# Modulation gates taken as columns through DRAM, six score sets, and Q/K weights loaded in column parts

## The chip, the cores and the metric

One Trainium2 chip, one core of it. The metric is the device time of one execution in microseconds (us). The executions of a kernel are compared with executions of the kernel before on the same chip in the same rounds.

The engines: TensorE (PE, with its weight loads PEld), VectorE (DVE), ScalarE (ACT), GpSimd (POOL), and SyncE (SP), which here issues all transfers (DMA) in one queue, in order (q1 on the pages: 50946 of the 50990 packets of the kernel before).

## The reference, cut to what matters

Shapes: `x` is 1 x 2048 x 640, 32 heads of 20, a causal window of 256, feed-forward width 1536, all bf16.

```python
mod = (silu(c) @ w_mod).reshape(1, 6, 1, 640)
sa, ca, ga, sb, cb, gb = (mod[:, i] for i in range(6))
h = layernorm(x) * (1 + ca) + sa
x = x + ga * attention(h, wqkv, wo)          # ga: the first gate
h = layernorm(x) * (1 + cb) + sb
x = x + gb * ((sigmoid(h @ w_gate) * (h @ w_up)) @ w_down)   # gb: the second gate
```

Two of the six modulation vectors are gates. The kernel multiplies them into the weights `wo` and `w_down`. For that each gate must stand as one row of 640, repeated on all 128 partitions (`gbc`).

Of the kernel before, what the change touches and what calls it, by code (L numbers as in the profile page):

```python
# [13 lines left out]
D = 640  # L14
H = 32
DH = 20
# [10 lines left out]
ENGS = ("pe", "act", "dve", "pool", "sp")  # L27

# [21 lines left out]
class Tile:  # L50
# [18 lines left out]
    @property  # L69
    def ap(self):  # L70
        return self.pool.aps[self.slot]

# [6 lines left out]
class Prog:  # L79
# [69 lines left out]
    def schedule(self):  # L149
# [35 lines left out]
        while placed < n:  # L185
# [62 lines left out]
            if o.isdma:  # L248
# [8 lines left out]
                hbm = max(acc + 0.8, hbm) + o.nbytes / 300e3  # L257
# [36 lines left out]
    def emit(self):  # L294
# [72 lines left out]
    "": "290 430 340 608 722 1953 1410 1740 303 468 448 570 1053 1093 711 721 823 490 280 320 510 -476 -138 -724 "  # L367
        "-544 -539 -489 -71 134 716 878 906 1114 630",
    "dma": "192",
    "x0": "-493",  # L370
    "x1": "122",
    "wm0": "289 373 247 331 163",
    "wqk": "593 396 748 863",
    "x2": "458",
    "x3": "571",
    "wv": "655",
    "warm": "1688 1731 1808 1817 1860 1903 608 651 694 2096 2118 1733 1755 1777 2206 2358 2303 2246 2268 2290",
    "c": "495",
    "modc": "715 854 921 802 892 636 867 881 894 907",
    "pad": "3909 5019",  # L380
    "stats@l0": "513 601 1331 1473",
    "aggr@l0": "2080 2100 2841 2972",
    "eps@l0": "570 1327",
    "pow@l0": "-460 1299",
    "xh@l0": "581 712 1726 1402",
    "ptr@l0": "645 747 685 403 767 1330 1387 1279 1412 1259",
    "hT0@l0": "-1511 -1721 -2114 -2170 -1702 -1156 -1042 -850 -674 -894",
    "projd@q0": "1459 1470 1482 1494 1506 1237 1305 1415 1444 1491 1823 1518 1340 1435 1447 1293 1341 1352 1352 "
        "1399 1518 1589 1601 1590 1625 2666 2618 2630 2642 2571 1951 1963 1974 1986 1998 2426 2437 2429 2441 2550 "
        "2526 2511 2535 2355 2665 3078 3090 3336 3113 3125 3206 3336 3348 3359 3371 3451 3494 3553 3581 3577 3218 "  # L390
        "3230 3241 3253 3265 3483 3589 3193 3632 3644 3420 3506 3518 3530 3542 3277 3289 3300 3312 3324",
    "evd@q0": "2246 1511 2380 1296 2117 3495 4441 3413 3670 3148 3408 4055 3755 4850 3604 3508",
    "projv0@q0": "2260 2288 1873 1900 1213 1644 2741 2766 3764 3791 3668 3856 4701 4729 4525 4553",
    "evv@q0": "2354 2393 1710 2835 1322 1753 3711 4640",
    "projq0@q0": "2687 2709 2129 2151 2074 2096 2238 2329 2019 2041",
    "evqk@q0": "990 1105 925 1294 996 1338 1786 1967 1544 1160",
    "qkw@q0": "3031 2588 2554 2692 2363 2752 3157 3354 2856 2528",
    "qkr@q0": "3818 3083 3041 3524 3860 3571 3609 3693 3567 3399 3545 3686 3902 3944 3776 4139",
    "projk0@q0": "2361 421 2810 2832 2990 3012 2482 2258 2184 2206",
    "wo@w": "5221 1685 2696 2459",  # L400
    "x4@l1": "1684",
    "x5@l1": "-3",
    "x6@l1": "1246",
    "x7@l1": "3007",
    "stats@l1": "2240 2112 1966 2328",
    "aggr@l1": "423 516 255 -869",
    "eps@l1": "2142",
    "pow@l1": "3115",
    "xh@l1": "4779 4659 4831 2815",
    "ptr@l1": "3146 3045 2947 2887 2864",  # L410
    "hTe@l1": "2501 1738 2392 2111 4012",
    "wm1@w": "2662 1477 2296 3998 3038",
    "modb@w": "5742 5769 6219 6194 9058 9085 9030 9126",
    "@w": "4934 5232 6126 8243 8298 8559",
    "modc@w": "6315 6328 6302 6457 6368 9167 9189 9422 9478 9491",
    "wos@w": "6411 6577 6699 6833 6728",
    "wm2@w": "7685 7139 7415 7878 6150",
    "wg@w": "9448 4001 8420 3092 5176 9902 4628 9836 9534 8922",
    "projq1@q1": "3934 4020 3977 4085 5851 5936 4888 4838 6069 6112",
    "evqk@q1": "3777 4175 6139 4611 5808 4684 4738 5207 5034 5620",  # L420
    "qkw@q1": "4228 4290 6482 4014 6064 4471 4208 5263 5164 5741",
    "qkr@q1": "6890 7188 6349 6092",
    "projk1@q1": "4327 4477 4243 4286 5074 5117 4769 4944 5455 5521",
    "projv1@q1": "5714 5810 3720 3747 4231 4452 5402 5429 6892 7082 6288 6578 6001 6416 5182 5209",
    "evv@q1": "4642 3829 4662 5328 7148 6250 6241 7971",
    "x8@l2": "3314",
    "x9@l2": "3422",
    "x10@l2": "3048",
    "x11@l2": "3443",
    "stats@l2": "3891 4057 3646 3734",  # L430
    "aggr@l2": "4037 4165 3871 4145",
    "eps@l2": "4247",
    "pow@l2": "4171",
    "xh@l2": "4506 4626 4486 4217",
    "ptr@l2": "5227 5028 4898 5341 5475",
    "hTe@l2": "1073 908 666 1262 1783",
    "score0@a0": "1587 1795 2920 3179 3392 3665 3841 3869",
    "exp0@a0": "1694 1895 3065 3145 3184 3341 3892 4158",
    "mask0@a0": "4936 3068 3790 3335 4505 4438 4716 4628 3044 2925 3411 2747 3019 3203 5634 5399",
    "pv0@a0": "3432 3463 3601 4187 4620 4640 5283 5302",  # L440
    "tr1@a0": "5924 6672 7198 7764",
    "recip@a0": "3621 4407 5110 4826",
    "divide@a0": "3979 4364 4932 5660",
    "tr2@a0": "4185 4710 4919 6259",
    "n_ow@a0": "5213 6164",
    "oT@a0": "6082 6356 6361 6345",
    "score1@a1": "4404 4669 5018 5331 5596 5245 5528 5800 6736 7022 7312 7614",
    "exp1@a1": "4449 4393 5090 5124 5510 6070 6380 6445 6882 7427 7533 7834",
    "mask1@a1": "4743 5195 5262 5195 5418 5835 4866 5475 5761 5641 6444 6173 6522 6399 6332 6367 6748 6682 6939 "
        "7006 7526 7100 7288 7192 7551 7460 7507 7740 8042 7976 8109 7387",  # L450
    "pv1@a1": "5628 5530 5556 6368 6412 6438 7546 7553 7579 7807 7833 8171",
    "tr1@a1": "5386 5962 7203 7796",
    "recip@a1": "4011 4674 6196 6643",
    "divide@a1": "5752 6555 7709 8385",
    "tr2@a1": "5958 6916 7740 8448",
    "n_ow@a1": "7195 8682",
    "oT@a1": "9194 9236 10033 9163",
    "wd@w": "12285 10761 11898 11749 12135 10910",
    "wds@w": "12996 12902 10989 10990 12482 12308 12113 11826 12880 13137 11378 11361",
    "x0@o0": "5965",  # L460
    "x1@o0": "6847",
    "wo0@o0": "7054 7191 7344 7029 7123 7150 7900 7927",
    "res1@o0": "7130 7632 7232 7943",
    "stats@o0": "7846 8181",
    "aggr@o0": "7925 8208",
    "eps@o0": "8321",
    "pow@o0": "9688",
    "xh@o0": "8529 8729",
    "transp@o0": "8417 8754",
    "modu@o0": "8694 9092 9256 8648 8699",  # L470
    "mlpg0@m0": "10485 10507 10678 10700 10865 10914 11728 11141 11403 11425 11513 11535 11665 11895 12392 12676 "
        "12168 12452 12206 12562 12586 12749 12836 12962",
    "mlpu0@m0": "10616 10638 10726 10748 10942 10962 11167 11189 11451 11483 11603 11625 11971 11993 12291 12382 "
        "12478 12575 12665 12687 12631 12653 12899 12921",
    "tanh@m0": "7042 7268 7797 11349 10492 11023 11809 11844 12141 12143 11761 12611",
    "glu@m0": "10926 10599 8433 11355 11611 11767 12164 12064 10375 10683 10350 10944",
    "down0@m0": "13436 13545 13678 13732 13787 14083 12989 13141 13490 13195 11887 11941",
    "res2@m0": "13250 13519 13183 13201",
    "out@m0": "13049 12362",
    "x2@o1": "4105",  # L480
    "x3@o1": "9866",
    "wo1@o1": "9957 9984 10240 10575 10880 11094 9482 11171",
    "res1@o1": "8885 9322 9602 9782",
    "stats@o1": "8874 9750",
    "aggr@o1": "11300 11788",
    "eps@o1": "12157",
    "pow@o1": "11951",
    "xh@o1": "12415 12471",
    "transp@o1": "13000 12774",
    "modu@o1": "12818 13129 13489 13438 13432",  # L490
    "mlpg1@m1": "13962 14048 14595 14617 15103 15125 15587 15609 16496 16230 16359 16381 16476 14690 14820 16667 "
        "16739 16761 16977 16989 17128 17150 17219 17293",
    "mlpu1@m1": "14481 14596 15097 15066 15154 15176 16214 16297 16314 16336 16544 16566 16634 16656 16744 16766 "
        "16983 17005 17092 17156 17244 16315 16453 15824",
    "tanh@m1": "13668 14197 14019 15261 15826 16069 16094 16320 16359 16578 16821 16672",
    "glu@m1": "14177 14047 14044 15218 15965 16207 16804 16480 16687 16752 16927 16694",
    "down1@m1": "16373 17507 17895 17950 18004 18210 17389 17689 17744 17798 18059 18113",
# [194 lines left out]
def build(nc, A_x, A_wqkv, A_wo, B_x, B_w_gate, B_w_up, B_w_down, c, w_mod, out, S=2048):  # L692
# [55 lines left out]
    def R(name):  # L748
        return Res(name)
# [69 lines left out]
    for b in range(2, 4):  # L819
        x0[b] = load_x(p_x0, b, 0.31 + 0.001 * b)  # L820
# [618 lines left out]
```

## The kernel before: the parts that the change touches

The kernel is a list of operations with read and write sets. A small list scheduler in the kernel file, with a cost model and a table of priorities, places them on the five engines when the kernel is built; the order on each engine is then fixed. A gate is made by multiplying `silu(c)`, repeated over 128 columns (`silubc`), with the columns of `w_mod`: every partition gets the same row, so nothing has to be broadcast afterwards.

```python
def mod_bc(wm, c0, factor, prio):
    for half in range(2):
        ps = Tile(p_M, "modb")
        pairs = [(ps[:, 0:320], silubc[:, kt, :], wm[:, kt, c0 + half*320 : +320]) for kt in range(5)]
        pe_chain(ps, 320, pairs, ...)                       # 5 matmuls of 320 columns
        gbc[:, half*320 : +320] = ps * factor               # VectorE
# ... shifts and scales are made as columns, [128, 5]:
def mod_cols(wm, c0, ps, prio):                             # w_mod is the stationary side
    for kt in range(5):
        for cg in range(5):
            mm(ps[:, cg*64 : +64], wm[:, kt, c0 + cg*128 : +128], silubc[:, kt, 0:64])
# ... the first Q/K weights come in two halves of 320 columns:
def load_wqk(half):
    for w in (wq, wk): dma(w[:, :, half*320 : +320], wqkv_src[...])
# ... [cut]: the scores of the first chunk go through exp in eight sets of 384 columns
```

(The code is abridged: index arithmetic and arguments are cut.)

The softmax here doesn't subtract the row's maximum and nothing guards it: scores larger than these inputs give would overflow.

## Time and profile before

| kernel before | |
|---|---|
| median of 6 runs, lowest and highest | 343.79 us, 342.9 to 345.37 |
| span of the profiled execution | 339.9 us |
| TensorE busy | 97% |
| TensorE's share of the chain that ended last | 92% |
| transfers under 512 bytes | 16513 of 50990 packets |

How to read it: the span is cut into 40 equal slices; a digit is the busy share of a slice in tenths (9 is 90% or more), and for PEclk the clock granted to TensorE in tenths of full speed. In the views, L864 is a line of kernel.py, often that of a helper. `x` are input blocks, `hT` and `h2T` the normalised inputs transposed (attention, feed-forward), `stg` results on their way out, `dq`, `dk` and `doc` the copies of Q, K and the attention output in DRAM, `QT`, `KT` and `oT` what is read back of them, `big` w_mod and later the products of the feed-forward, `wgu` w_gate and w_up, `wd` w_down.

```profile
PE   7799989999999999998999999999999999999996
...
PEclk9999999999999999999999999999999999999999
```

TensorE is full from end to end (97% busy) and its clock does not drop (1.00 granted up to the last matmul).

### The profile page before, as it was taken

The page shows a single profiled execution, that of the slowest core. Times are in us where ns is not written, and L with a number is a line of the kernel's source. Part 1 is how long each engine was busy: PE and PEld are TensorE (multiplying, and loading weights), DVE is VectorE, ACT ScalarE, POOL GpSimd, SP SyncE. Part 2 cuts the span into 40 slices and gives each one's busy share as a digit, 9 for nine tenths or more (in the row PEclk, how much of TensorE's full clock was granted, in tenths as well). Part 3 has the DMA queues.
Part 4 walks back from the last instruction along what each step waited for, and adds up shares of the span by engine and source line. Part 5 has one row for each costly group of instructions (what it writes and reads, how often), then busy time and mean ns, then how long its engine had stood idle before and what let it go on. Part 6 is the DMA issues. An engine that isn't in the chain of part 4 may idle for free.

```text
span 339.9 us, 9584 instructions
## 1 busy us (share of the span) xinstructions
PE 330.0 (97%) x3813; PEld 201.2 (59%) x3813; DVE 227.6 (67%) x493; ACT 226.9 (67%) x229; POOL 178.4 (52%) x301
## 2 busy tenths in 40 slices
PE   7799989999999999998999999999999999999996
PEld 2577646655555656564765433466545446788884
DVE  4576599999776889646977446398746874554432
ACT  1377878888888888896887798956678851022230
POOL 5132564797666999555675566656656850010000
PEclk9999999999999999999999999999999999999999
DMA  6966689889987752472064101302740122112101
GB/s 211 353 202 181 191 235 257 288 270 209 231 282 253 224 194 41 151 226 60 2 180 115 48 31 65 111 3 40 162 123 12 49 22 72 44 35 41 39 3 39
DMA packets 50990, 44.99 MB, mean 132 GB/s; under 512 B 16513, under 2 KB 46850, under 8 KB 50946
## 3 DMA queue, kind: packets, MB, share of 16 engines
q1 hardware_dynamic: 50946, 44.38, 45.4%
q8 instruction: 30, 0.49, 0.6%
q14 instruction: 14, 0.11, 0.1%
HBM read 28.90 MB, written 12.19 MB: 121 GB/s over the span
## 4 chain that ended last, share of the span: by engine, by line
PE 92%; DMA 4%; SPq 1%; DVE 1%; ACT 1%; issue 0%; ACTq 0%; DVEq 0%
PE M L842 74%; PE S L843 8%; PE O L843 7%; PE M L843 3%; DMA big<-in_w_mod_dram 2%; DMA oT<-doc 1%; SPq L764 1%; DMA doc<-On 1%; ACT hT L984 0%; DVE x L937 0%; DVE V L1020 0%; DVE hT L1005 0%; ACT stg L1019 0%; DVE x L1316 0%; DVE big L1306 0%
## 5 line engine op out<-in xcount | busy, mean ns | idle before, releaser
L1188 ACT ACTIVATE E<-S 128x2048 bf16<-128x2048 f32 (+1 forms) x64 | 118.0, 1844 | 20.9 <-PE S L843 19.6
L842 PE MATMUL M<-h2T,wgu 128*128 128x256 bf16 (+1 forms) x720 | 114.6, 309 | 0.0
L842 PEld LDWEIGHTS M<-h2T,wgu 128*128 128x128 bf16 x720 | 67.2, 98 | 36.6 <-issue 5.5
L1199 POOL TENSOR_SCALAR_AFFINE_SELECT E<-E 128x512 bf16<-128x512 bf16 x89 | 59.9, 683 | 23.3 <-ACT E L1188 21.6
L1201 POOL TENSOR_SCALAR_AFFINE_SELECT E<-E 128x512 bf16<-128x512 bf16 x78 | 50.4, 655 | 31.8 <-ACT E L1188 27.5
L1306 DVE SCALAR_TENSOR_TENSOR big<-sig,M 128x256 bf16<-128x256 f32 (+1 forms) x72 | 36.4, 506 | 41.7 <-PE M L842 20.2
L1304 ACT ACTIVATE sig<-M 128x256 f32<-128x256 f32 (+1 forms) x72 | 32.4, 452 | 44.1 <-PE M L842 43.5
L842 PE MATMUL M<-wd,big 128*128 128x320 bf16 x384 | 56.5, 299 | 0.0
L842 PEld LDWEIGHTS M<-wd,big 128*128 128x128 bf16 x384 | 36.5, 98 | 16.0 <-issue 1.7
L843 PE MATMUL S<-QT,KT 20*128 20x256 bf16 (+2 forms) x832 | 36.2, 258 | 0.0
L926 DVE BATCH_NORM_STATS2 st<-x 128x6 f32<-128x320 bf16 x64 | 27.3, 477 | 7.2 <-DMA x<-in_A_x_dram 7.1
L1249 DVE STREAM_TRANSPOSE T<-O 128x512 f32<-128x512 f32 x32 | 22.6, 708 | 12.6 <-PE O L843 12.5
L843 PEld LDWEIGHTS S<-QT,KT 20*128 20x128 bf16 x832 | 12.3, 92 | 26.5 <-ACT E L1188 9.4
L1316 DVE TENSOR_TENSOR x<-M,x 128x320 bf16<-128x320 f32 x32 | 15.5, 484 | 18.3 <-PE M L842 17.8
L842 PE MATMUL M<-wv,hT 128*128 128x320 bf16 x160 | 27.4, 300 | 0.0
L842 PE MATMUL M<-wo,oT 128*128 128x320 bf16 x160 | 25.8, 300 | 1.5 <-DMA oT<-doc 1.4
L932 POOL TENSOR_SCALAR st<-st 128x2 f32<-128x2 f32 (+1 forms) x11 | 3.0, 274 | 40.4 <-DVE st L929 40.4
L842 PE MATMUL M<-hT,wk 128*128 128x512 bf16 (+1 forms) x100 | 23.1, 354 | 1.1 <-DVE V L1020 1.0
L1258 DVE STREAM_TRANSPOSE On<-Tn 128x512 bf16<-128x512 bf16 x32 | 22.5, 704 | 0.5
L842 PE MATMUL M<-hT,wq 128*128 128x512 bf16 (+1 forms) x100 | 22.7, 356 | 0.0
L843 PE MATMUL O<-E,V 128*32 128x256 bf16 (+2 forms) x568 | 21.1, 262 | 0.0
L1019 ACT ACTIVATE stg<-M 128x512 bf16<-128x512 f32 (+1 forms) x31 | 16.5, 534 | 6.6 <-PE M L842 6.2
(85 smaller groups left out, 386.3 us busy)
## 6 DMA issues: line engine op xcount, KB each, us to landing
x<-in_A_x_dram SPq DMA_DIRECT2D x32, 160.0 KB, 4.1
big<-in_w_mod_dram SPq DMA_DIRECT2D x15, 320.0 KB, 5.5
doc<-On SPq DMA_DIRECT2D x16, 256.0 KB, 2.2
KT<-dk SPq DMA_DIRECT2D x6, 512.0 KB, 5.1
QT<-dq SPq DMA_DIRECT2D x6, 512.0 KB, 4.7
out_dram<-x SPq DMA_DIRECT2D x16, 160.0 KB, 1.8
wgu<-in_B_w_gate_dram SPq DMA_DIRECT2D x5, 384.0 KB, 4.1
dq<-stg SPq DMA_DIRECT2D x15, 128.0 KB, 3.2
```

The source lines that it names most:

```text
L842: return e.matmul(o, l, r, start=st, stop=sp, skip_group_check=True)
L843: return e.matmul(o, l, r, start=st, stop=sp, tile_position=tp, skip_group_check=True)
L926: ins = e.bn_stats(v(bi * 12 + j * 6, 6), src[bi].ap[:, j * 320:(j + 1) * 320])
L1019: return e.activation(dst(), src(), ACT.Copy)
L1188: A("act", lambda e, eng, E=E, Sp=Sp, ncol=ncol: e.activation(E.ap[:, :, 0:ncol], Sp.ap[:, :, 0:ncol], ACT.Exp, scale=SM_SCALE), c_act(4 * ...
L1199: return e.affine_select(ap, ap, pattern=[[0, 4], [1, 128]], compare_op=ALU.is_ge, fill=0.0, base=0, channel_multiplier=-1)
L1201: return e.affine_select(ap, ap, pattern=[[0, 4], [-1, 128]], compare_op=ALU.is_ge, fill=0.0, base=-1, channel_multiplier=1)
L1249: A("dve", lambda e, g: e.transpose(T1.ap[:], O.ap[:]), 0.71, reads=[O.r()], writes=[T1.r()], prio=4, tag="tr1")
L1258: A("dve", lambda e, g: e.transpose(On.ap[:, half * 512:half * 512 + 512], Tn.ap[:]), 0.71, reads=[Tn.r()], writes=[On.r(half)], prio=7, t ...
L1304: A("act", lambda e, g, pg=pg, sg=sg: e.activation(sg.ap[:, 0:W], pg.ap[:, 0:W], ACT.Tanh, scale=0.5), c_act(W), reads=[pg.r()], writes=[s ...
L1306: A("dve", lambda e, g, pu=pu, sg=sg, ft=ft: e.scalar_tensor_tensor(out=hv(ft), in0=sg.ap[:, 0:W], scalar=1.0, in1=pu.ap[:, 0:W], op0=ALU. ...
L1316: A("dve", lambda e, g, ps=ps, bi=bi, half=half: e.tensor_tensor(x1[bi].ap[:, half * 320:half * 320 + 320], ps.ap[:, 0:320], x1[bi].ap[:, ...
```

## The change

Its intent: take work from TensorE and from the head of the kernel. (1) Both gates are made as columns like the shifts and scales (25 matmuls of 64 columns in place of 10 of 320), and a transfer to DRAM and back turns the column into a broadcast row. (2) The scores of the first chunk go through exp in six sets of 512 columns in place of eight of 384. (3) The first Q/K weights come in three column parts. (4) The modulation columns use PSUM banks that belong to the scores and are free at that time. (5) The priorities were searched anew, with a cost model that got a DRAM bandwidth for each kind of transfer.

```diff
+    CUTS = [0, 172, 332, D]
+    def load_wqk(part):
+        c0, c1 = CUTS[part], CUTS[part + 1]          # ... one wq and one wk transfer for each part
...
     def mod_bc(wm, c0, factor, prio):
-        for half in range(2):
-            ... five matmuls of 320 columns, then gbc[:, half] = ps * factor on VectorE
+        gd = dram(f"gate{c0}", [D])
+        col = mod_cols(wm, c0, ps, prio)
+        A("dve", ... tensor_scalar(gcol[:], col(), factor, None, op0=ALU.mult) ...)
+        dma(gd.rearrange("(t p) -> p t", p=128), gcol[:], 1280, ..., nd=640, tag="gw")
+        dma(gbc[:], bass.AP(gd.tensor, gd.offset, [[0, 128], [1, D]]), 163840, ..., tag="gr")
...
-    psA, psA2 = Tile(p_M, "modA"), Tile(p_M, "modA2")
+    psA, psA2 = Fixed(p_S.aps[0][:, 1, :], "psA"), Fixed(p_S.aps[0][:, 2, :], "psA2")
...
+        if a == 0:    # six score sets, three for each four groups of heads
...
 TIMES = { ... all priorities replaced ... }
```

`gcol` is [128 partitions, 5], and element (p, t) goes to place 128 t + p of one run of 1280 bytes: 640 single elements of 2 bytes.

## The prediction

> **What bounds the kernel now.** I read the page first: busy time by engine, then the chain that ended last.
>
> ```profile
> span 339.9 us, 9584 instructions
> PE 330.0 (97%) x3813; PEld 201.2 (59%) x3813; DVE 227.6 (67%) x493; ACT 226.9 (67%) x229; POOL 178.4 (52%) x301
> ...
> PE 92%; DMA 4%; SPq 1%; DVE 1%; ACT 1%; issue 0%; ACTq 0%; DVEq 0%
> ```
>
> TensorE (PE) is the bound: 97% busy, 92% of the chain, every other engine at two thirds or less. So a part of the change counts only if it alters what PE executes, or how long PE waits. "Busy" says nothing of density, so next I took the timeline of PE in its undisturbed end and divided durations by counts.
>
> ```profile
> 10.40 1.34 PE L842 MATMUL M<-silubc,big 128*128 128x64 bf16 x40 [1.01 <-DMA big<-in_w_mod_dram]
> ...
> 318.06 12.50 PE L842 MATMUL M<-h2T,wgu 128*128 128x256 bf16 x113
> 330.39 6.68 PE L842 MATMUL M<-wd,big 128*128 128x320 bf16 x48
> ```
>
> Start to start (a run's length less the tail of its last matmul) this gives 29 ns for 64 columns, 109 ns for 256, 136 ns for 320, and in other rows 216 ns for 512. The small tiled matmuls (scores, P times V, direct projection) run four at a time, and where PE goes over between full-array, row-tiled and column-tiled work, the start of the next piece comes some 100 ns later than these figures (312 instead of 216 ns after a 512-column matmul). I summed counts by these figures: 294.8 us of work without warm-up, and 237 changes of tiling at 0.1 us = 23.7 us. That is 318 of 340 us. The rest: 13.2 us before the first projection (1.9 us of listed work lies there), 2.8 us after the last matmul, and waits of PE. The waits view of PE names them:
>
> ```profile
> PE M L842 <- DMA big<-in_w_mod_dram: 2.0, 2, 1.0
> PE M L842 <- DMA oT<-doc: 1.4, 1, 1.4
> PE M L842 <- DVE V L1020: 1.4, 2, 1.0
> ```
>
> They are few and short: the two for w_mod lie before 13 us, the one for oT at 156 us, those for DVE at 18 and 49 us. So all that can be gained by better order after 13 us is some 4 to 5 us of named waits plus about 3 us of diffuse loss: at most 2%.
>
> [...] the trace before holds no such transfer, so the cost of the new one is open. [...] the new 172-column weight part has rows of 344 B, and no run yet shows what that costs here.
>
> **The change, part by part.**
>
> *Gate as columns.* Removed: 20 matmuls of 320 columns (two gates, two halves, five steps), 20 x 0.136 = 2.7 us. Added: 50 of 64 columns, 50 x 0.029 = 1.45 us. PE saves 1.27 us. In return the gate goes out to DRAM as 640 single elements and comes back broadcast. The first gate is ready at about 56 us of PE work and the scaled wo is needed at 77: hidden. The second is discussed below.
>
> *Six score sets.* 8 sets of 384 columns become 6 of 512: same matmuls and columns. ACT saves 8 x 1.447 - 6 x 1.877 = 0.3 us of exp, off the path.
>
> *New order.* The built program's order on PE has 249 changes of tiling against 237: +1.2 us. With the saving above, PE's own work is unchanged (-0.1 us). The gain is not in work; only waits decide.
>
> *Head.* A third x block now goes ahead of four of the five w_mod pieces. w_mod's last piece landed at 10.36 us and releases everything; 164 KB more at about 300 GB/s is +0.5 us. The freed M banks let the transposes run without the 0.3 and 0.5 us waits at 12.0 and 12.65, and column parts remove the need of a whole half of the weights, but the first wait was for w_mod, not for weights: part loading hides what was hidden. The part of wk with columns 0 to 171 is now even the last to be loaded, at about 18.6 us by the same bytes; it is first used at about 19.5. Waits between 13 and 50 us: 2.5 us before; the new order stretches the evictions differently, and I take half of it as gone: -1.2 us.
>
> *oT of the third chunk.* Before, dk writes and a 512 KB QT read stand around doc and oT in the queue, and oT lands 12 us after the last PV. Now doc goes out at once and no QT read lies between. PE does 10.3 us of other work in between; I expect about 10 us needed: 1.4 of wait becomes about 0.2, -1.2 us.
>
> *w_mod behind a transpose.* This is the bad part. The DMA queue takes its issues in order, and a waiting issue holds all behind it.
>
> ```profile
> 84.74 0.58 SPq L764 DMA_DIRECT2D big<-in_w_mod_dram  x1
> 85.36 0.50 SPq L764 DMA_DIRECT2D wgu<-in_B_w_gate_dram  x1
> 86.27 1.23 SPq L943 DMA_TRANSPOSE h2T<-x  x1
> ```
>
> Before, the last w_mod piece of the third set goes ahead of the h2T transpose. In the new program it stands behind the first h2T transpose, which waits for the LayerNorm of the first chunk after its output projection. Before, 5.1 us passed from the last of those projections (81.2 us) to that transpose (86.27). Add 1.25 us for its issue and 4.5 us for w_mod to land (median of five, 3.5 to 5.5): 10.9 us. The new order on PE leaves 6.9 us of work between that projection and the matmul that reads this piece. That is a new wait of up to 4 us near 100 us; a quicker LayerNorm chain (DVE has fewer casts between) and an emptier queue could halve it. I put +2.2 us. Behind it the second gate's write, its read back and one w_up piece stand in a row; PE has some 9.7 us for what needs 9 to 10: +0.3 us.
>
> *Tail.* The last output is stored in two halves; the transfer after the last residual carries 80 KB instead of 160 KB. Of the 2.8 us after the last matmul most is latency: -0.2 us.
>
> Sum: -0.1 + 0.5 - 1.2 - 1.2 + 2.2 + 0.3 - 0.2 = +0.3 us. Against 344.02 that is 344.3 us.
>
> **Rivals.** *The order is simply better:* the queue model in the source got per-kind bandwidths, which speaks for a search that sees DMA landings better; then the 100 us wait is small and the early waits vanish: -4 us, 340. Against it: 92% PE in the chain leaves no more. *The queue bites harder:* both the w_mod wait and the gate's round trip show in full, and the late wk part as well: +2, +2, +1 us more, 349. For it: DMA is at 92% of its time between 58 and 100 us, and 640 single-element writes go through the same engines. *Early exp starvation:* the first scores come some 11 us later (27 instead of 16 us of PE time), so exps could become the bound: 62 sets x (1.88 + about 0.5 us) = 148 us spread over 246 us of score time. ACT has room; 0 us.
>
> **Range and chances.** The certain terms nearly cancel; the two big waits have errors of about 2 us each, the early waits 1.5 us, and the three timings of before spread by 2.5 us. That gives 344.3 with 340 to 348.5 for 8 in 10. 2% is 6.9 us: faster would need nearly all named and diffuse waits gone without a new one; slower would need both queue waits at their worst and something I have not seen.
>
> **What would show it.** PE's unit costs and 97% busy should stay; the 320-column silubc group should be gone and a 64-column one of 150 stand in its place. PE should wait for w_mod once near 100 us for 1 to 4 us, and hardly for oT near 155. The first direct projection should start at about 13.5 us. If there is no wait near 100 us, the LayerNorm chain was quicker than I read it, and the time falls to about 342. If PE's share of the span drops below 95%, a wait I have not named rules.

## The result, and the profile after

**378.48 us** median of six runs (376.43 to 379.71), against 343.79 us before. The ratio is 1.0994, 95% interval 1.0948 to 1.104: slower by 10%. (A ratio is the mean time of one kernel's fast runs over that of the other's fast runs of the same rounds, so it is not quite the ratio of the medians.) The prediction of 344.3 us, 340 to 348.5, was wrong.

The page of the changed kernel, with the lines that answer to those shown of before:

```profile
span 376.6 us, 9615 instructions
...
PE 333.3 (89%) x3816; PEld 201.2 (53%) x3843; DVE 229.5 (61%) x489; ACT 227.6 (60%) x228; POOL 179.4 (48%) x302
...
PE   7789989906987816999999999999999999999997
...
PEclk9999999986999975999999999999999999999999
...
PE 62%; DMA 21%; DVE 7%; SPq 4%; POOL 3%; issue 2%; ACT 1%; DVEq 0%; POOLq 0%
```

TensorE's work is as large as before, but it now fills only 89% of the span, and transfers hold 21% of the chain (4% before). The slices show where: two holes, at the ninth and the fifteenth slice (a slice is 9.4 us), and a lower clock in and after each. The waits view of TensorE (what was waited for, us in total, times, longest):

```profile
PE M L864 <- DVE stg L1043: 12.1, 2, 11.8
PE M L864 <- DMA wgu<-in_B_w_up_dram: 11.2, 1, 11.2
...
PE M L864 <- DMA big<-in_w_mod_dram: 1.4, 2, 0.8
```

Two waits make 23 us. The second names a transfer. The first names a cast on VectorE, but that cast only stood in line: the chain (start, us, what) passes through it to a transfer of x that took 20 us, where such a block took 4.1 us in the kernel before (median of 32).

```profile
65.29 20.19 DMA x<-in_A_x_dram
...
87.28 0.56 DVE stg L1043
...
87.89 0.71 PE M L864 x10
```

What stood beside that transfer is seen in the queue of issues (start, us taken by the issue, line, transfer):

```profile
64.07 0.51 SPq L782 DMA_DIRECT2D gate<-gcol  x1
65.29 1.31 SPq L783 DMA_DIRECT2D x<-in_A_x_dram  x3
...
85.33 0.34 SPq L783 DMA_DIRECT2D gbc<-gate  x1
...
122.58 0.38 SPq L782 DMA_DIRECT2D gate<-gcol  x1
...
138.32 0.33 SPq L783 DMA_DIRECT2D gbc<-gate  x1
138.70 0.42 SPq L783 DMA_DIRECT2D wgu<-in_B_w_up_dram  x1
```

The read-back `gbc<-gate` waits for the write of the gate. It could only be issued 21.3 us after the first write (the queue issued nothing from 71.0 to 85.33 us), and 138.32 - 122.58 = 15.7 us after the second, for 1280 bytes. The second wait of TensorE comes through the queue: the chain goes from the write (122.58 us) to the read-back and from there to the w_up piece that was issued just behind it at 138.70 us, landed 5.2 us later and let TensorE go on at 144.06. At the first gate the x transfers had been issued ahead of the read-back and were slow all the same: the write isn't alone in being slow. The DMA view of the stretch from 64 to 86 us (40 slices of 0.55 us; busy share in tenths, then GB/s):

```profile
DMA  9989999999999000025644262748939399559465
GB/s 339 245 284 302 333 335 303 339 240 91 41 59 26 0 0 0 0 30 90 65 30 16 13 57 77 64 43 37 26 9 28 9 30 52 51 49 90 112 126 113
...
x<-in_A_x_dram SPq DMA_DIRECT2D x4, 160.0 KB, 16.8
KT<-dk SPq DMA_DIRECT2D x1, 512.0 KB, 16.0
```

For 2 us nothing moves at all, then 9 to 126 GB/s where it had been about 300. The second KT read had been issued just ahead of the gate's write (the two from 63.0 us on) and still took 16 us. In the records of single packets the 640 elements look harmless: 640 packets of 2 bytes for each write, 9 ns each (median; 28 ns at most), all gone within 2 us (67.2 to 68.9 us and 123.6 to 125.6 us). But packets of over 600 bytes behind them are on record with up to 10.7 us.

Each stall costs more than its length. The timeline of TensorE around the second one, and the clock in that place (windows view: stretch, length, busy us of the engines, then the granted clock):

```profile
132.41 0.40 PE L865 MATMUL O<-E,V 128*32 128x256 bf16 x8
144.06 4.00 PE L864 MATMUL M<-h2T,wgu 128*128 128x256 bf16 x18 [11.24 <-DMA wgu<-in_B_w_up_dram]
```

```profile
88.00:90.00 2.00, 1.78 (x29) 0.97 (x30) 2.00 (x7) 0.00 (x0) 1.41 (x1) 0.50 0.71 211
90.00:92.00 2.00, 2.00 (x21) 1.37 (x21) 1.48 (x5) 1.88 (x1) 2.00 (x5) 0.67 0.78 235
...
144.00:146.00 2.00, 1.94 (x10) 1.41 (x11) 1.05 (x4) 0.04 (x1) 0.23 (x1) 0.50 1.08 372
146.00:148.00 2.00, 2.00 (x14) 1.15 (x12) 1.12 (x3) 0.35 (x1) 2.00 (x2) 0.50 1.69 260
148.00:150.00 2.00, 2.00 (x25) 1.05 (x25) 0.14 (x1) 1.19 (x2) 0.83 (x1) 0.66 0.69 160
```

Eighteen matmuls of 256 columns in 4.00 us are 222 ns each, twice the 109 ns of the undisturbed end: the clock is at half. A mean of 0.67 or 0.66 over 2 us is, if the clock is either half or full there, half clock for two thirds of it, so half clock lasted 2 + 1.3 = 3.3 us after the first stall and 4 + 1.3 = 5.3 us after the second. With finer borders the windows view has 0.50 from 87.89 to 91.30 us and from 144.06 to 149.35 us, and 1.00 behind both. Half of that is lost: 4.3 us. What sets these lengths was not shown.

The remaining lines that answer to those of the prediction, in two views. The timeline of TensorE: the 64-column group now on score banks, and the undisturbed end with the same unit costs (12.94 us for 117 against 12.50 us for 113):

```profile
10.06 1.10 PE L864 MATMUL S<-silubc,big 128*128 128x64 bf16 x26 [0.28 <-DMA big<-in_w_mod_dram]
...
354.24 12.94 PE L864 MATMUL M<-h2T,wgu 128*128 128x256 bf16 x117
```

The queue: the w_mod piece behind the h2T transpose, as the prediction had read it from the program:

```profile
115.29 0.42 SPq L783 DMA_DIRECT2D wgu<-in_B_w_gate_dram  x1
115.75 1.24 SPq L966 DMA_TRANSPOSE h2T<-x  x1
117.03 0.58 SPq L783 DMA_DIRECT2D big<-in_w_mod_dram  x1
```

### The profile page after: what moved, and what is told of

It is laid out like the page before. It is cut to its first block, busy times and chain, and to the rows that moved or that the text cites. A ratio compares the mean times of both kernels' runs of the same rounds, so it can differ in the third digit from the quotient of the medians.

```text
span 376.6 us, 9615 instructions
## 1 busy us (share of the span) xinstructions
PE 333.3 (89%) x3816; PEld 201.2 (53%) x3843; DVE 229.5 (61%) x489; ACT 227.6 (60%) x228; POOL 179.4 (48%) x302
## 4 chain that ended last, share of the span: by engine, by line
PE 62%; DMA 21%; DVE 7%; SPq 4%; POOL 3%; issue 2%; ACT 1%; DVEq 0%; POOLq 0%
PE M L864 51%; DMA x<-in_A_x_dram 7%; PE S L865 5%; PE O L865 4%; DMA gate<-gcol 4%; SPq L783 4%; DMA wk<-in_A_wqkv_dram 3%; DMA wd<-in_B_w_down_dram 1%; DMA wgu<-in_B_w_up_dram 1%; PE M L865 1%; DMA h2T<-x 1%; DMA big<-in_w_mod_dram 1%; DVE st L949 1%; POOL E L1224 1%; DMA oT<-doc 1%
## 5 line engine op out<-in xcount | busy, mean ns | idle before, releaser
L1211 ACT ACTIVATE E<-S 128x2048 bf16<-128x2048 f32 x64 | 120.1, 1877 | 40.8 <-PE S L865 33.8
L864 PE MATMUL M<-h2T,wgu 128*128 128x256 bf16 (+1 forms) x708 | 114.6, 311 | 14.8 <-DMA wgu<-in_B_w_up_dram 11.2
L1224 POOL TENSOR_SCALAR_AFFINE_SELECT E<-E 128x512 bf16<-128x512 bf16 x91 | 61.2, 681 | 33.3 <-ACT E L1211 31.1
L1226 POOL TENSOR_SCALAR_AFFINE_SELECT E<-E 128x512 bf16<-128x512 bf16 x80 | 52.2, 662 | 35.6 <-ACT E L1211 34.8
L865 PE MATMUL S<-QT,KT 20*128 20x128 bf16 (+2 forms) x832 | 36.2, 260 | 1.0 <-ACT E L1211 0.9
L864 PE MATMUL M<-wo,oT 128*128 128x320 bf16 x160 | 26.7, 300 | 1.2 <-DVE x L1308 0.9
L864 PE MATMUL M<-wv,hT 128*128 128x320 bf16 x160 | 27.3, 300 | 0.1
L864 PE MATMUL M<-hT,wk 128*128 128x512 bf16 (+1 forms) x91 | 21.4, 352 | 2.3 <-DVE st L952 0.5
L865 PE MATMUL O<-E,V 128*32 128x256 bf16 (+2 forms) x588 | 22.4, 263 | 0.5 <-POOL E L1226 0.4
L1042 ACT ACTIVATE stg<-M 128x512 bf16<-128x512 f32 (+1 forms) x28 | 15.0, 535 | 10.8 <-PE M L864 6.0
```

Of the source, the lines that this page charges most:

```text
L864: return e.matmul(o, l, r, start=st, stop=sp, skip_group_check=True)
L865: return e.matmul(o, l, r, start=st, stop=sp, tile_position=tp, skip_group_check=True)
L1211: A("act", lambda e, eng, E=E, Sp=Sp, ncol=ncol: e.activation(E.ap[:, :, 0:ncol], Sp.ap[:, :, 0:ncol], ACT.Exp, scale=SM_SCALE), c_act(4 * ...
L1224: return e.affine_select(ap, ap, pattern=[[0, 4], [1, 128]], compare_op=ALU.is_ge, fill=0.0, base=0, channel_multiplier=-1)
L1226: return e.affine_select(ap, ap, pattern=[[0, 4], [-1, 128]], compare_op=ALU.is_ge, fill=0.0, base=-1, channel_multiplier=1)
```

## The experiments

The theories, as they stood before the runs. **1:** the write of single elements holds up the transfers around it; in three forms, by a price for each small descriptor, that is, for each contiguous piece that the transfer moves (1a; the trace of the changed kernel has one packet for each of the 640 elements), for any small write whatever its number (1b), or because many writes fall into the same short stretch of DRAM (1c). **2:** the new order of instructions costs the time. **3:** any write with a dependent read-back in the in-order queue costs it.

The scheduler plans anew whenever an operation's modelled cost changes, and then many instructions change places on every engine. So most experiments keep the order: either the modelled cost stays as it was and only an address pattern changes (the built programs were compared and differ in nothing but the transfer named), or the placement is written out as a list in the kernel file and replayed with the entries named put in or moved (called "frozen" below). Where that wasn't done, it is said. Fourteen kernels ran; all but the three marked so give right results.

### The write made harmless, nothing else touched

```diff
-gd.rearrange("(t p) -> p t", p=128)  <-  gcol[:]            # 640 x 2 bytes
+gd.rearrange("(t p) -> t p", p=128)  <-  ident[0:5, :]      # 5 x 256 bytes; wrong on purpose
```

> Instruction order of the changed kernel on all five engines exactly as it is; only the gate's write to DRAM takes five rows of 256 bytes from the identity tile in place of 640 elements of 2 bytes from the gate columns (the result is wrong on purpose; the write still waits for the gate columns, the read-back still waits for the write). Theory 1, the write of single elements blocks the transfers: both stalls of TensorE of 11.8 and 11.2 us and the lower clock after them go, time 345 to 350 us, read-back issued within 4 us of the write's issue. Theory 2, the new order of instructions (weights in column parts, six sets, scheduler's plan) is what costs: stays above 370 us. Theory 3, any dependent write and read-back in the transfer queue costs this: above 360 us, with the read-back still more than 10 us behind the write.

Measured: 349.42 us, ratio 1.0157 (1.0111 to 1.0203). Both stalls are gone and the clock of the profiled execution is 1.0 throughout. Queue, second gate:

```profile
107.81 0.28 SPq L782 DMA_DIRECT2D gate<-ident  x1
...
110.67 0.41 SPq L783 DMA_DIRECT2D gbc<-gate  x1
```

The read-back follows after 2.9 us in place of 15.7 (after 5.8 us at the first gate, so "within 4 us" was missed there; other entries stand between). The order of all instructions is the changed kernel's to the last one, so theory 2 falls for 29 of the 35 us, and so does theory 3, as the dependent round trip is still there. What is left, 5.6 us, is looked at further down.

### The gate in runs of ten bytes

```diff
-stationary = wm[:, kt, c0 + cg*128 : c0 + cg*128 + 128];  gd "(t p) -> p t" <- gcol    # 640 x 2 bytes
+stationary = wm[:, kt, c0 + cg : c0 + 640 : 5];           gd "(p t) -> p t" <- gcol    # 128 x 10 bytes
```

> Same order; the gate's weight columns are taken with stride 5, so that a partition of the gate columns holds five neighbouring outputs and the write has 128 descriptors of 10 bytes in place of 640 of 2 bytes; right result. Theory 1a, the cost goes with the number of small descriptors: the write's block falls from 16 to 21 us to a fifth, 3 to 5 us, and the time to 346 to 353 us. Theory 1b, any small write near others in DRAM costs the same whatever their number: above 370 us. Theories 2 and 3: above 360 us.

Measured: 353.02 us, the upper edge of the range, 1.0245 (1.0184 to 1.0307); read-back 7.8 and 4.1 us after the writes. 1b falls. A fifth of the descriptors takes away nearly all of the block, but that fits 1a and 1c alike.

### Single elements, but spread out

```diff
-gd = dram("gate", [640]);      gd "(t p) -> p t" <- gcol
+gd = dram("gate", [640 * 32]); gd "(t p s) -> p t s"[:, :, 0] <- gcol    # every 64 bytes
-gbc <- gd, broadcast
+gbc <- first row of wqkv, broadcast (still waits for the write; wrong on purpose)
```

> Same order and still 640 elements of 2 bytes, but each element 64 bytes from the next in DRAM (the read-back takes a row of another tensor, so the result is wrong on purpose). Theory 1a, a price per small descriptor wherever it lands: unchanged, 375 to 382 us. Theory 1c, writes that fall into the same short stretch of DRAM wait for each other: the block is nearly gone, 345 to 355 us.

Measured: 349.78 us, 1.016 (1.0124 to 1.0195), as with five rows. Still 640 descriptors of 2 bytes, in the same queue, in the same order; only their distance in DRAM is different. Theory 1a falls, 1c stands. A later run with 8 bytes of distance (32 replaced by 4, wrong too):

> The changed kernel, same order, elements of 2 bytes 8 bytes apart in DRAM, so eight to every 64 bytes in place of 32 (wrong result on purpose, as with 64 bytes). If what counts is how many writes fall into the same 64 bytes: about a quarter of the block, second read-back released about 6 us after the write (15.7 in the changed kernel, 2.9 with 64 bytes between), time 350 to 356 us. If what counts is a larger stretch of DRAM, all 640 elements still lie within 5 KB: above 12 us and above 368 us.

Measured: 353.76 us (350.18 and 352.03 in the two fast runs), 1.0218 (1.0164 to 1.0272), second read-back 4.5 us after the write. So all 640 within 5 KB do little harm, and how densely they lie is what counts. How long the stretch is that counts, 64 bytes or some hundreds, these runs don't tell: a quarter of the density is a quarter of the number in any stretch up to the 1280 bytes of the dense write. In one profiled execution each, the block shrinks faster than the number in it: from 32 to 8 elements in 64 bytes, the excess over the spread-out write (2.9 us) falls from 12.8 to 1.6 us, an eighth for a quarter.

### The gate made as before, in the changed kernel

```diff
-mod_bc: 25 matmuls of 64 columns, gcol, write, read-back
+mod_bc: ten matmuls of 320 columns, gbc = ps * factor        # planned anew by the scheduler
```

> The changed kernel with its gate made as before (ten broadcast matmuls of 320 columns for each gate, no DRAM); the scheduler plans anew, so the order around both gates differs. Theory 1: no stall over 3 us at the two places, time 344 to 352 us; what is left above the kernel before is the head, measured at about 3 us in the changed kernel. Theory 2: above 365 us, since six sets, column parts and placement of PSUM are all still in.

Measured: 353.96 us, 1.0291 (1.0245 to 1.0336). The two long stalls are gone, as theory 1 had it, but the time lies 2 us above its range. The scheduler had to plan another order for these operations, and nothing here tells whether it is that order or the broadcast that costs more. This run can't be used to set the price of anything small, and it is why the order is frozen in the runs that follow.

### One gate alone, in the kernel before

Second gate only, order of the kernel before frozen:

```diff
-second gate: ten matmuls of 320 columns, gbc = ps * factor
+second gate: 25 matmuls of 64 columns, gcol
+queue: gate <- gcol (640 x 2 bytes) behind the four oT transfers; gbc <- gate five entries later
```

> The kernel before with one part of the change alone: its second gate by 25 column matmuls and the DRAM round trip with 640 elements of 2 bytes, the write issued just behind the four oT transfers of the second chunk; order of everything else frozen to that of the kernel before. Theory 1 (the element write into one short stretch of DRAM holds up the transfers behind it): 352 to 362 us, with the read-back released 12 to 17 us after the write and a stall of TensorE of several us on a transfer that was issued behind it. Theory 2 (it is the new order or the weights in parts): 343 to 345 us, as neither is in this kernel.

Measured: 359.77 us, 1.042 (1.0364 to 1.0477). One gate's write is enough for 16 us, with no weights in parts, no six sets and no new order. Read-back 15.8 us behind the write. TensorE:

```profile
108.89 1.49 PE L844 MATMUL M<-wo,oT 128*128 128x320 bf16 x5 [8.24 <-DMA oT<-doc]
118.96 2.30 PE L844 MATMUL M<-hT,wq 128*128 128x512 bf16 x5 [3.01 <-DMA dq<-stg]
```

The oT transfers stood ahead of the write in the queue and were held up all the same. Now one could still say that it is the queue of issues that stands at the read-back. So the read-back was put eight entries later (the expectations say ten; the edit has eight):

```diff
 queue: gate <- gcol (640 x 2 bytes); wgu; wgu; x; wgu
-       gbc <- gate
        x; dq; wgu; doc; QT; x; wd; wd
+       gbc <- gate
        QT; KT; ...
```

> As f1_before_one_gate (640 elements of 2 bytes), with the read-back at the same later place as in f3_10b_later_read. Rival: only the queue of issues stands still at the read-back, the other transfers are not touched; then the time falls to that of f3, 343 to 346 us. Theory 1, the write itself blocks the transfers already behind it: they still land 10 us and more after their issue, TensorE stalls for several us, 350 to 360 us.

Measured: 359.51 us, 1.0471 (1.0431 to 1.0511): nothing gained. DMA view of 96 to 120 us of this run (slices of 0.6 us):

```profile
GB/s 203 168 79 72 10 0 5 102 67 20 31 31 15 26 67 31 36 46 26 36 46 61 61 31 36 15 41 35 115 304 405 385 378 429 374 336 142 32 82 193
```

The write was issued at 96.32 us, and some 17 us pass until the rate is back. In this kernel the place of the read-back plays no part, and the standing queue falls as the whole cause for the 2-byte write. (In the changed kernel it was still the way by which the second stall came about, as seen above.)

### What a better write would have given

The same two kernels with ten-byte runs, f2 with the early and f3 with the late read-back, and a third one (f5) with proper rows: TensorE turns the five columns with one matmul by the identity, VectorE copies them to bf16, and five rows of 256 bytes are written, late read-back.

```diff
-gd "(t p) -> p t" <- gcol
+ps[0:5, 384:512] = gcol.T @ ident        # one matmul
+grow = ps[0:5, 384:512]                  # VectorE, to bf16
+gd "(t p) -> t p" <- grow                # 5 x 256 bytes
```

> The same as f1_before_one_gate, but with the gate's columns taken with stride 5, so that the write has 128 runs of 10 bytes; right result. Theory 1: 343 to 345 us (the saving of ten matmuls of 136 ns against 25 of 29 ns is 0.6 us), read-back released 3 to 5 us after the write. A round trip that costs by itself would give above 347 us.

> As f2_before_one_gate_10b (the kernel before with its second gate by columns, 128 runs of 10 bytes), but the read-back stands ten entries later in the queue of transfers, behind the first two w_down pieces, so that nothing useful stands behind a wait for the write. If the 5.2 us that f2 lost came from the queue standing still at the read-back (it was issued 4.8 us after the write): 342.5 to 345 us, no wait for a dq transfer near 108 us. If the write itself still holds up other transfers: 346 us or more.

> The kernel before, order frozen, second gate by columns, turned on TensorE into five rows and written as five rows of 256 bytes, read back at the later place of f3_10b_later_read; right result. If f3's 4.3 us were still the small writes in one stretch of DRAM (its longest packet behind the write took 3.3 us, against 0.9 us behind rows): 342.5 to 344.5 us, no wait for a dq transfer near 109 us. If column gates cost time through anything else in the round trip: 346 us or more.

Measured: f2 349.12 us, 1.0113 (1.0064 to 1.0162); f3 347.64 us, 1.0105 (1.0062 to 1.0149); f5 345.67 us, 1.0023 (0.9981 to 1.0065). f2 came out above its range, where its rival stood (above 347 us), and f3 in the range for a write that still holds up others (346 us or more): ten-byte runs aren't harmless. f5 fell between its two ranges (up to 344.5, from 346 us). f3 shows that the early read-back wasn't the reason, because TensorE waits for the same transfer; f5 shows that the round trip isn't either, as only 0.6 us of that wait is left:

```profile
109.17 1.91 PE L844 MATMUL M<-hT,wq 128*128 128x512 bf16 x4 [2.79 <-DMA dq<-stg]
```

```profile
105.53 1.25 PE L845 MATMUL M<-hT,wq 128*128 128x512 bf16 x5 [0.58 <-DMA dq<-stg]
```

(first f3, then f5). Not all of the excess need be this wait: near 160 us the profiled executions wait for oT too, 2.2 us in f2, 2.8 in f3 and 2.1 in f5 against 1.4 in the kernel before. In f2 the cost of such a wait is raised by the clock: behind a wait of 2.29 us five matmuls of 512 columns took 2.30 us in place of 1.27, and the granted clock was 0.50 over the first 1.60 us and 0.57 over the next 2.00, another 1.7 us lost by my estimate (0.50 x 1.60 + 0.43 x 2.00). The windows view has

```profile
108.40:110.00 1.60, 1.60 (x5) 0.51 (x6) 0.00 (x0) 0.00 (x0) 0.89 (x2) 0.50 0.43 133
```

With rows the column gate is level with the kernel before (the interval goes from -0.2% to +0.7%). The 0.6 us of TensorE work that it saves isn't visible. So no version here beats the kernel before.

The packet records put the writes side by side. "Longest" is the longest time of one packet over 600 bytes within 14 us of the write's issue, "moved" is what all engines moved in these 14 us. In the kernel before, the same place (96.3 us) has 1.3 us and 3.8 MB without any such write.

| second gate's write | run | longest packet, us | moved, MB |
|---|---|---|---|
| 640 x 2 bytes, dense | after; f1; f4 | 5.4; 6.7; 8.0 | 1.1; 0.7; 0.7 |
| 128 x 10 bytes, dense | e1; f2; f3 | 3.4; 3.5; 3.3 | 3.2; 3.1; 3.0 |
| 640 x 2 bytes, 8 bytes apart | e2_padded_8_bytes | 2.4 | 3.0 |
| 640 x 2 bytes, 64 bytes apart | e2_padded_64_bytes | 1.1 | 3.2 |
| 5 x 256 bytes | e4; f5 | 1.1; 1.1 | 3.1; 3.6 |

### The rest: 5.6 us over the kernel before

First the changed kernel made right with rows, as in f5 (frozen):

> The changed kernel, order frozen, repaired so that the result is right: the five gate columns are turned by one TensorE matmul with the identity into five rows of 128, copied to bf16 by VectorE, and written as five rows of 256 bytes; two matmuls and two small copies more. Theory 1: as with the identity rows, 347 to 352 us. If the write from gate columns itself were not the cause (for example the wait on VectorE in front of it), above 360 us.

Measured: 352.49 us, 1.0233 (1.0163 to 1.0303), 0.5 us above its range. Then three moves in the queue (the x block's two statistics move along on VectorE):

```diff
-oT x4; wgu; h2T transpose; w_mod piece 4 of the third part; h2T transpose
+w_mod piece 4 of the third part; oT x4; wgu; h2T transpose x2
-x2 first of all; ...; wk part 2; wq part 2
+...; wk part 1; x2; ...; wq part 2; wk part 2
```

> As e4_rows_right, with three moves in the order of transfers and nothing else: the last piece of the third w_mod part is issued ahead of the four oT transfers of the second chunk as in the kernel before (it stood behind an h2T transpose), the third x block behind w_mod and the first wk part, with its two statistics on VectorE, and the wq columns 332 to 639 ahead of the wk columns 332 to 639. If what is left over the kernel before, about 5.5 us, is these places of the order: 1.5 to 4 us less than e4_rows_right, the wait for w_mod near 101 us gone and the wait near 19 us under 0.5 us. If the rest comes from elsewhere (TensorE work, six sets): within 1 us of e4_rows_right.

Measured: 350.47 us (350.05 by its three fast runs), 1.0154 (1.0099 to 1.0208): 2.4 us less by the medians of fast runs, within the expected band, though the intervals of both overlap. The wait near 19 us went (2.0 us in e4), but one of 0.8 us for wk came up at 16.4 us. One of the waits for w_mod went, another stayed, with 1.4 us at 102 us. Two more moves, and one on top of that on VectorE:

```diff
 e7: queue:   two more w_mod pieces ahead of the last hT transpose; two w_up pieces ahead of the gate's write
 e8: VectorE: -hT modulation x3; residual addition
              +residual addition; hT modulation x3
```

> As e5_rows_head_wm2, with two more moves in the order of transfers: the second and third of the last four w_mod pieces ahead of the last hT transpose of the fourth chunk, and two w_up pieces ahead of the second gate's write, at which the queue stood 4 us for VectorE's row copy. If what is left is places in the queue: the wait for w_mod near 102 us (1.4) and for w_up near 119 us (2.0) go, 346 to 349 us; otherwise within 1 us of e5_rows_head_wm2 at 350.5.

> As e7_rows_queue_places, with one move on VectorE: the residual addition that TensorE waited 3.6 us for stands ahead of the hT modulations instead of behind their wait for the hT transposes. If what is left over the kernel before is made of such places in the in-order engines: 346 to 348.5 us and that wait gone. If each wait taken away comes back elsewhere: within 1 us of 350.5 us.

Measured: e7 350.93 us (350.13 by its three fast runs), 1.0192 (1.0144 to 1.024); e8 352.14 us, 1.0223 (1.0163 to 1.0283). Both missed what was hoped for: e7 is within 1 us of e5, its other range, and e8 lies above both of its ranges. e7's profiled execution fell in the slow state, so no reading here rests on its trace; but the 3.6 us in e8's expectation were read from it. In e8 the wait that was to go is gone, and the next residual addition holds TensorE, and then the clock is down for over 5 us:

```profile
98.35 2.33 PE L865 MATMUL M<-hT,wk 128*128 128x512 bf16 x5 [2.45 <-DVE x L1314]
```

```profile
98.40:100.00 1.60, 1.60 (x4) 0.55 (x5) 1.02 (x4) 0.00 (x0) 0.37 (x2) 0.50 1.00 292
100.00:102.00 2.00, 2.00 (x19) 0.43 (x18) 1.29 (x3) 0.73 (x1) 2.00 (x4) 0.50 0.98 216
102.00:104.00 2.00, 2.00 (x9) 0.79 (x7) 0.57 (x1) 1.15 (x1) 1.22 (x3) 0.50 0.65 159
```

Where the rest lies can be told, if not what its root is. I added up, matmul by matmul, what the start of the next one came later than the unit cost and 0.1 us for a change of tiling:

| us lost in the stretch | before | e6 (after, harmless write) | e8 |
|---|---|---|---|
| 0 to 30 us | 6.3 | 6.9 | 7.0 |
| 30 to 90 us | 1.9 | 2.5 | 2.6 |
| 90 to 120 us | 0.1 | 5.7 | 7.0 |
| 120 us to the end | 1.8 | 1.9 | 2.6 |
| sum | 10.1 | 16.9 | 19.1 |

The difference of the sums, 6.8 us, is nearly that of the spans (346.9 and 339.9). Nearly all of it lies between 90 and 120 us, where the hT and h2T transposes, the last w_mod pieces, the second gate and the w_up weights come together, and where taking one wait away brought another. That the new order is looser there is shown; which one step of it is the root stays open.

## Why the prediction was wrong

Its reading of the kernel before held: TensorE is the bound, only waits decide. Its last test was right too: "If PE's share of the span drops below 95%, a wait I have not named rules." Point by point:

- **Gate as columns, TensorE's work.** Right by count: the changed kernel has 64-column matmuls at the same unit cost (29 ns start to start, in both traces), and f5 with one gate is level with before. But the saving is too small to be seen.
- **First gate "hidden".** This is the step that failed. It asked when the gate is needed, and not what its write does to others. The write at 64.07 us cost 11.8 us of TensorE and some 1.6 us of half clock. The prediction had said itself, of the write of single elements, that "the cost of the new one is open" and then booked it at zero. An unknown was entered as a point.
- **Second gate, +0.3 us.** The same failure, but here only a size was wrong and not the path: the w_up piece did stand behind the write and its read-back, as the prediction had it. The write took 15.7 us (2.9 with rows), and that made 11.2 us and some 2.6 us of half clock of the 0.3. Both gates together: 23.0 + 4.3 = 27.3 us of the 29.1 us between the changed kernel and e6.
- **Rival "the queue bites harder".** Right in kind, with the single elements named as its reason, and wrong in size: +2 us for the gate against 29. It pictured the wait for the round trip. That is how the second stall came about, but not the first, where transfers issued ahead of the read-back stood still; and f4 shows that moving the read-back away gains nothing.
- **w_mod behind the transpose, +2.2 us.** The place in the queue is as read, and the wait is there, but the size is too large: the matmuls that need this last piece waited 0.6 us (at 121 us; 0.4 in e6), and e5, which moves the piece, has no such wait. Another wait for w_mod close by (0.8 us; 1.1 in e6, and 1.4 in e5 in spite of the move) wasn't in the prediction.
- **What the sum didn't have.** e6 shows 5.7 us lost between 90 and 120 us, where the prediction had 2.2 + 0.3. The waits named there are 1.5 us for w_mod, 1.4 for VectorE's residual additions, which stand behind hT modulations that wait for their transposes, 0.9 for exps on ScalarE and 0.8 for w_up. The prediction looked for waits at transfers only, and not for an in-order engine between a transfer and TensorE.
- **Head, +0.5 us, and early waits, -1.2 us.** The first direct projection started at 13.01 us against 13.20: -0.2, not +0.5. The early waits didn't shrink but grew: 0 to 90 us lost 9.4 us in e6 against 8.2. The wk part with columns 0 to 171 was used at 23.0 us, not 19.5, and TensorE waited 0.5 us for it. The waits that it meant to halve were also read too large: the waits view of the kernel before names 1.4 us between 13 and 50 us, not 2.5, and 2.8 us in all after 13 us, not "4 to 5".
- **oT of the third chunk, -1.2 us.** In the changed kernel the wait is 0.3 us against 1.4 before, as predicted. But in e6, with the same order and no stalls, it is 1.1, so the agreement may be luck.
- **Six sets, -0.3 us on ACT, no exp starvation.** No starvation in the first chunk. But TensorE waited 0.9 us for exps, all of it between 113 and 120 us, where the kernel before has no such wait. The 0.3 us isn't visible (ACT busy 227.6 against 226.9 us).
- **Tail, -0.2 us.** Right: the span ends 2.6 us after the last matmul, 2.8 before (of which the last transfer's packets ran for some 0.6 us).

With a cost for the write as measured, 344.3 + 29 = 373; the other 5 us are those by which e6 lies above 344.3. The range was too narrow by its own account: a transfer of a kind that the trace had never shown deserved a tail of tens of us, not 2.

## What to carry to other kernels

Before a small result goes through DRAM, count how densely its separate writes lie (here 32, 8 and 1 in 64 bytes gave the block, little of it and none: the second read-back was issued 15.7, 4.5 and 2.9 us after the write), and turn it into rows on TensorE first. Space between the elements helped too, but was only run with a read-back of another tensor; what reading spaced elements costs wasn't measured. A transfer that is off the critical path can still hold up those beside it (here the rate fell from about 300 to between 0 and 126 GB/s), so ask what it does to its neighbours and not only when its result is needed. With a nearly full TensorE the waits of 2.29 us (f2) and 2.45 us (e8) were paid about twice, by the clock: it stood at 0.50 behind them, which took another 1.7 and 2.9 us by my estimate from the windows views. And to compare orders, freeze them: a scheduler that plans anew moves more than the part under test.

## What the runs show of small writes and of the clock

- Small writes to DRAM held up other transfers: 640 dense writes of 2 bytes (1280 bytes in all) took 15.7 to 21.3 us until a dependent transfer was released, and in the 14 us after one of them (f1, f4) all engines together moved 0.7 MB in place of 3.8 MB.
- Size alone isn't what hurt: 640 writes of 2 bytes at 64 bytes distance cost nothing that these runs could see (349.8 us against 349.4 us with five rows), dense ones 29 us. No run shows the mechanism: the elements themselves are on record with 9 ns each, and only the packets behind them with up to 10.7 us.
- Gaps of TensorE of 2.29 us (f2) and 2.45 us (e8) were followed by a clock of 0.50 for some 3 and over 5 us. In e8 TensorE was thinly used before the gap as well (busy 0.55 of the 3.4 us from 95.0 to 98.4 us); in f2 it had been busy throughout from 104 us to the gap.
